# Attention beside a feed-forward block on one core: the normalisation of U moves from VectorE to GpSimd, V in two copies, 36 exp blocks, a new order

## The chip, the cores and the metric

The kernel runs on 1 core of one Trainium2 chip. The metric is the time of one execution on the device in microseconds (us), median of 3 runs. A core has five engines that matter here: TensorE (matmuls into PSUM, an accumulator memory of 8 banks), ScalarE, VectorE, GpSimd and SyncE (which issues most DMAs). In the profile they are PE, ACT, DVE, POOL and SP; PEld is the loading of weights into TensorE.

## What is computed

The input x has 2048 rows of 640. It is normalised over its rows, and the result xn goes into two branches: attention with 32 heads of 20 that share one key and one value head, and a feed-forward block of width 1728 with SiLU. Both are added to x.

```python
def _A_ref(x, wq, wk, wv, wo):
    B, S, D = x.shape
    H = 32
    Dh = D // H
    q = (lambda x, *d: x.transpose(*d))((x @ wq).reshape(B, S, H, Dh), 0, 2, 1, 3)
    k = x @ wk
    v = x @ wv
    scores = jnp.einsum("bhqd,bkd->bhqk", q, k) * (Dh ** -0.5)
    p = _softmax(scores, axis=-1)
    o = jnp.einsum("bhqk,bkd->bhqd", p, v)
    return (lambda x, *d: x.transpose(*d))(o, 0, 2, 1, 3).reshape(B, S, H * Dh) @ wo
...
xn = _layernorm(x, axis=-1)
return x + _A_ref(xn, A_wq, A_wk, A_wv, A_wo) + _B_ref(xn, B_w1, B_w2)
```

## The kernel before

**Blocks, groups, steps.** The scores are computed transposed, in blocks of 128 keys by 512 queries of one head. There are 4 stages of 512 queries, 32 heads and 16 blocks of keys: 2048 blocks. Four heads form a group (32 groups in all, g), and the four heads of a group stand on four tiles of 32 rows of TensorE's array, so that four small matmuls run side by side. A score step (do_S, matmuls on L1127) makes three or four blocks, each in a PSUM bank of its own.

**Two ways to take the exponential.** ScalarE reads one, two or three neighbouring banks in one instruction (L1161) and writes exp to blocks of the buffer E, of which there are NBLK = 35. VectorE reads one bank (L1176) and uses a linear approximation: added to an offset and stored as a 16-bit integer, the score becomes the bit pattern of a bf16 number Z that is close to the exponential. One such reading is coarse, so three are averaged: Z itself and Z with its bits shifted by 43 and by 86, weighted 1, 0.8046875 and 0.625. The two shifts are integer additions on GpSimd (INT64_ADD, L1202, in flush_z), over up to ZB = 3 blocks in one instruction; they write to Y, which has 4 places of two. The weights lie in V, which therefore stands in three copies.

**Weighted sums.** do_pv (L968) multiplies the blocks by V, four tiles side by side, and accumulates a group in one PSUM bank. A block from ScalarE is one matmul; a block from VectorE is three, one for each of its readings. V has one column more that gives the sum of the weights.

**End of a group.** VectorE copies the bank to U (L1245), SyncE transposes U with a DMA to UT (L1216, norm_dma), and normalise takes the reciprocals of the sums on VectorE (L1231) and multiplies (L1236, 128x320) into o. For the last of the 32 groups the transpose is done on TensorE instead. When a stage's groups are done, DMAs on SyncE transpose o to oT (try_oT) for the output projection.

**The rest.** Queries, feed-forward and output projections run as jobs between the score steps (mm4, L870). The hidden layer takes a tanh on ScalarE (L1336) and a product on VectorE (L1341); sums are read on L1405, L1412, L1424. In the opening x is loaded and normalised, keys and values are projected, and VectorE writes the copies of V (L1804, one instruction for each copy and each four row tiles). GpSimd's memsets prepare V (L1597, L1599).

**The order.** All instructions are put in order when the program is built, by a planner (Sched and step) that gives each operation a duration and takes on each engine the ready one of lowest priority number. Each engine then works strictly in that order and waits on semaphores. For an operation of n numbers that VectorE reads from PSUM the planner counts n/960 + 0.067 us, also for the multiplication of normalise; for an addition of n blocks on GpSimd YP_FIX + YP_BLK n. A table SEG holds 64 rows of planner settings, one for each 32 blocks. Among them are thresholds of VectorE's backlog below which it gets one or two blocks of a step (DVE_TH, DVE_TH2) and TILE_CAP, the most blocks of one tile (one head of a group) that VectorE may get.

Of the kernel before, what the change touches and what calls it, by code (L numbers as in the profile page):

```python
# [45 lines left out]
PH = ((0, 1.0), (43, 0.8046875), (86, 0.625))  # L46
# [4 lines left out]
NBLK = 35  # L51
# [53 lines left out]
YP_FIX = 0.147  # L105
YP_BLK = 0.218
# [13 lines left out]
            "ACT4", "SPLIT", "U2", "LOOK", "W4", "M3")  # L120
SEG = (
# [105 lines left out]
class Sched:  # L227
    def __init__(self, nc, stack):
# [12 lines left out]
        self.lock_end = {"dve": 0.0, "pool": 0.0}  # L241
        self.busy = defaultdict(float)
        self.last_add = None
        self.dmaq = defaultdict(float)

    def sem(self, name):
        self.nsem += 1
# [1635 lines left out]
```

## Time and profile before

| | us |
|---|---|
| median of 3 runs | 669.36 |
| lowest and highest | 669.29, 669.47 |
| the profiled execution's own time | 669.12 |
| its span, from the first to the last instruction | 667.3 |

The profile is of one execution. A group of instructions is shown as: line, engine, operation, what it writes and reads (partitions x numbers), count, total busy us, mean ns of one, and then the engine's idle time before them with what ended it. The view by stage gives, for stretches of the span, each engine's busy us with the count of its instructions, the granted clock of TensorE, the share of time in which the DMA engines were busy, and GB/s. The view of waits gives who waited for whom. The chain of waits is followed back from the last instruction and lists start, duration and what it was.

| line | engine | what |
|---|---|---|
| L1127 | PE | score matmuls |
| L1161 | ACT | exp readings |
| L1176 | DVE | exp readings by integers |
| L1202 | POOL | the two shifts of these |
| L968 | PE | weighted sums |
| L870 | PE | projections and feed-forward |
| L1236 | DVE | U times the reciprocals |
| L846 | PE | filling matmuls while nothing else is ready |

### The profile page before, as it was taken

The numbers are of one execution on the slowest core, as the hardware profiler recorded it, in microseconds if no ns is written. First come the engines' busy times: TensorE is split into PE (matmuls) and PEld (weight loads), VectorE is DVE, ScalarE is ACT, GpSimd is POOL, SyncE is SP. The second block draws the span as 40 slices with busy tenths as digits, with TensorE's granted clock in tenths as the row PEclk, the third lists the DMA queues.
The fourth block names the chain that finished last, engine by engine and source line by source line (L and its number), as shares of the span: only waits on it lengthen the run. The fifth ranks groups of instructions, "written<-read, shape, count | busy, mean of one in ns | idle before, by whom it ended". The sixth has DMA issues, their size and how long they took to land.

```text
span 667.3 us, 22800 instructions
## 1 busy us (share of the span) xinstructions
PE 659.4 (99%) x9735; PEld 220.4 (33%) x9735; DVE 601.3 (90%) x1085; ACT 647.7 (97%) x737; POOL 404.6 (61%) x509
## 2 busy tenths in 40 slices
PE   8999999999999999999999999999999999999998
PEld 4432233332323322233333323233233333223345
DVE  7888999999989999999889999988999999998783
ACT  7999999999999999999999999999999999999993
POOL 2056457777486656676556653866767674676550
PEclk9999999999999999999999999999999999999999
DMA  7565201010012210000003110000002121001001
GB/s 211 110 213 150 73 14 12 2 26 2 18 44 62 57 10 17 3 10 18 19 10 84 41 32 17 10 10 18 10 13 47 38 57 37 10 10 31 5 11 41
DMA packets 51433, 26.73 MB, mean 40 GB/s; under 512 B 38566, under 2 KB 50694, under 8 KB 51334
## 3 DMA queue, kind: packets, MB, share of 16 engines
q1 hardware_dynamic: 51190, 25.12, 14.5%
q8 instruction: 78, 1.28, 0.8%
q14 instruction: 21, 0.17, 0.1%
q10 hardware_dynamic: 144, 0.16, 0.1%
HBM read 11.44 MB, written 2.62 MB: 21 GB/s over the span
## 4 chain that ended last, share of the span: by engine, by line
PE 87%; ACT 7%; DVE 3%; SPq 1%; DMA 1%; issue 0%; ACTq 0%
PE psall L968 33%; PE psall L1127 28%; PE psall L870 26%; ACT sbt L1161 6%; DVE sbt L1176 2%; ACT sbt L1336 1%; SPq L1531 1%; DMA sbt<-in_A_x_dram 1%; DVE sbt L1424 0%; PE psall L1326 0%; DVE sbt L1236 0%; ACT sbt L1620 0%; DVE sbt L1666 0%; DVE sbt L1771 0%; ACT sbt L1655 0%
## 5 line engine op out<-in xcount | busy, mean ns | idle before, releaser
L1161 ACT ACTIVATE sbt<-psall 128x1024 bf16<-128x1024 f32 (+2 forms) x649 | 620.1, 1129 | 3.5 <-PE psall L1127 2.6
L1202 POOL INT64_ADD sbt<-sbt x492 | 399.7, 827 | 244.4 <-DVE sbt L1176 171.3
L1176 DVE TENSOR_SCALAR sbt<-psall 128x512 uint16<-128x512 f32 x732 | 473.1, 683 | 46.3 <-PE psall L1127 37.1
L968 PE MATMUL psall<-sbt 128*32 128x512 bf16 x3512 | 265.0, 383 | 0.2
L1127 PE MATMUL psall<-sbt 32*128 32x512 bf16 x2048 | 245.8, 384 | 2.1 <-ACT sbt L1161 0.7
L870 PE MATMUL psall<-sbt 128*32 128x320 bf16 (+2 forms) x3923 | 220.7, 331 | 0.5 <-DVE sbt L1176 0.4
L1127 PEld LDWEIGHTS psall<-sbt 32*128 32x128 bf16 x2048 | 61.9, 91 | 241.4 <-ACT sbt L1161 161.1
L870 PEld LDWEIGHTS psall<-sbt 128*32 128x32 bf16 x3923 | 84.6, 95 | 84.6 <-issue 54.4
L968 PEld LDWEIGHTS psall<-sbt 128*32 128x32 bf16 x3512 | 64.4, 95 | 101.3 <-issue 64.6
L1336 ACT ACTIVATE sbt<-psall 128x512 bf16<-128x512 f32 x54 | 39.6, 739 | 0.0
L1341 DVE SCALAR_TENSOR_TENSOR sbt<-sbt,psall 128x512 bf16<-128x512 bf16 x54 | 36.6, 682 | 2.6 <-ACT sbt L1336 1.2
L1245 DVE CAST sbt<-psall 128x512 bf16<-128x512 f32 x32 | 21.8, 681 | 5.4 <-PE psall L968 5.3
L1236 DVE TENSOR_TENSOR sbt<-sbt 128x320 bf16<-128x320 bf16 x31 | 18.3, 591 | 0.1
L846 PE MATMUL psall<-sbt 128*128 128x512 bf16 (+4 forms) x55 | 15.2, 428 | 1.2 <-DVE sbt L1590 1.2
L1424 DVE SCALAR_TENSOR_TENSOR sbt<-psall,sbt 128x320 bf16<-128x320 f32 x28 | 13.1, 477 | 2.9 <-PE psall L870 2.9
L1405 DVE SCALAR_TENSOR_TENSOR sbt<-psall,sbt 128x320 bf16<-128x320 f32 x28 | 13.5, 483 | 1.6 <-PE psall L870 1.4
L1294 DVE TENSOR_SCALAR sbt<-psall 128x512 bf16<-128x512 f32 (+1 forms) x19 | 12.9, 680 | 0.1
L1635 DVE BATCH_NORM_STATS2 sbt<-sbt 128x6 f32<-128x320 bf16 x22 | 10.0, 470 | 0.9 <-DMA sbt<-in_A_x_dram 0.7
L1421 ACT ACTIVATE sbt<-psall 128x320 bf16<-128x320 f32 x4 | 1.7, 438 | 8.7 <-PE psall L870 8.7
L846 PEld LDWEIGHTS psall<-sbt 128*128 128x128 bf16 x55 | 5.5, 109 | 9.1 <-issue 4.0
L1231 DVE RECIPROCAL sbt<-sbt 128x16 f32<-128x16 bf16 x31 | 7.5, 243 | 0.0
L1620 ACT ACTIVATE sbt<-sbt 128x640 bf16<-128x640 bf16 x5 | 3.6, 730 | 3.2 <-DMA sbt<-in_A_x_dram 3.2
(57 smaller groups left out, 70.1 us busy)
## 6 DMA issues: line engine op xcount, KB each, us to landing
sbt<-in_A_x_dram SPq DMA_DIRECT2D x32, 160.0 KB, 3.2
out_dram<-sbt SPq DMA_DIRECT2D x15, 160.0 KB, 2.0
sbt<-in_B_w_dram SPq DMA_DIRECT2D x5, 432.0 KB, 5.3
sbt<-sbt SPq DMA_DIRECT2D x105, 20.0 KB
sbt<-in_B_w_dram SPq DMA_DIRECT2D x13, 160.0 KB, 3.1
sbt<-sbt SPq DMA_TRANSPOSE x58, 2.5
sbt<-in_A_wo_dram SPq DMA_DIRECT2D x5, 160.0 KB, 3.1
sbt<-in_A_wq_dram SPq DMA_DIRECT2D x5, 140.0 KB, 3.1
```

The lines of the kernel that those rows point to most:

```text
L846: return pe.matmul(self.bk(b, 0, n), self.zero[:, 0:P], self.zero[:, 0:n], start=True, stop=True)
L870: ins = pe.matmul(self.bk(b, 0, n, r, r + SLOT), w[:, r:r + SLOT], x, start=start, stop=stop, tile_position=(0, r), skip_group_check=True)
L968: ins = pe.matmul(self.bk(ub[k], 0, QW, r, r + SLOT), self.v[:, it.w, it.kt, :], it.x(), start=f, stop=False, tile_position=(0, r), skip_g ...
L1127: ins = pe.matmul(self.bk(bank[x]), self.kT[r:r + SLOT, kt * P:(kt + 1) * P], self.qT[r:r + SLOT, g % QS, :], start=True, stop=True, tile_ ...
L1161: return a.activation(self.E[:, b0 * QW:(b0 + na) * QW].rearrange("p (b n) -> p b n", n=QW), src, AF.Exp, scale=ACT_SCALE)
L1176: return v.tensor_scalar(self.Z[:, zs, zp * QW:(zp + 1) * QW], self.bk(bb), OFF, ZMAX, ALU.add, ALU.min)
L1202: sc.new("pool", YP_FIX + YP_BLK * n, lambda g, k=k: g.int64_add(self.Y[:, ys, k, 0:w].bitcast(I64), self.Z[:, zs, 0:w].bitcast(I64), PH[k ...
L1236: sc.new("dve", t_dve_ps(16 * DH), lambda v: v.tensor_tensor(dst, ut[:, :, :, 0:DH], rb, ALU.mult), [key, ("rL", up)], [("o", h0 + i) for ...
L1245: sc.new("dve", t_dve_ps(QW), lambda v: v.tensor_copy(self.U[:, up, :], self.bk(ub)), [("B", ub)], [("U", up)], prio=U_PRIO, name=f"Uev{g}")
L1336: sc.new("act", t_act(QW), lambda a: a.activation(t, src, AF.Tanh, scale=0.5), [("B", b)], [("tb", tp)], prio=TH_PRIO, name=f"th{c}_{fk}") ...
L1341: sc.new("dve", t_dve_ps(QW), lambda v: v.scalar_tensor_tensor(out=self.hT[0:rows, fk, :], in0=t, scalar=1.0, in1=src, op0=ALU.add, op1=AL ...
L1405: sc.new("dve", t_dve_ps(320), lambda v: v.scalar_tensor_tensor(out=in1, in0=ps, scalar=0.5, in1=in1, op0=ALU.mult, op1=ALU.add), [("B", b ...
```

## The change

The three weights become two: both shifted readings have the weight 0.71875, their shifts are 39 and 82, and V stands in two copies. E gets one block more. The multiplication in normalise goes to GpSimd for all groups but the last, at priority 3.0, ahead of the additions at 4.0, with a planned duration of 1.0 us. Additions are planned at 0.159 + 0.222 n us in place of 0.147 + 0.218 n. There is new code that adds the two shifted readings to each other with an accumulating DMA, so that a block from VectorE has two matmuls in place of three; it is taken where GpSimd's planned backlog is under MG, and MG is a new column of SEG, 0 in all its rows. All 64 rows of SEG are new; the last of each is shown. The column TILE_CAP sums to 457 over the rows before and to 431 after; among these stand two values of 21 before and one after.

```diff
-PH = ((0, 1.0), (43, 0.8046875), (86, 0.625))
+SHIFT = (39, 82)
+VW = (1.0, 0.71875)
+NRM = 1.0
+NRM_PRIO = 3.0
...
+ACC_NEXT = (0.28, 0.22, 0.12)
+ACC_FROM = 78.0
+ACC_DMA = 0.0
+MG = 3.0
+MG_END = 16
...
-NBLK = 35
+NBLK = 36
...
-YP_FIX = 0.147
-YP_BLK = 0.218
+YP_FIX = 0.159
+YP_BLK = 0.222
...
-            "ACT4", "SPLIT", "U2", "LOOK", "W4", "M3")
+            "ACT4", "SPLIT", "U2", "LOOK", "W4", "M3", "MG")
...
-    (5.183, 0.388, 0.712, 0.335, 4, 1, 7, 2.4, 0.05, 2.683, 2.77, 8, 2.29, 0.835, 10, 7, 5, 54, 40, 33, 2, 0.2, 1, 0, 99, 0, 0, 1),
...
+    (7.286, 1.014, 0.096, 0.071, 1, 3, 1, 2.27, 0.05, 1.514, 2.65, 30, 2.29, 0.835, 10, 5, 25, 54, 30, 99, 99, 0, 1, 2, 12, 0, 0.5, 2, 0),
...
+        if e == "pool":
+            if op.dma:
+                self.after_acc = 0
+            else:
+                if self.after_acc < len(ACC_NEXT):
+                    op.dur += ACC_NEXT[self.after_acc]
+                self.after_acc += 1
...
-        self.v = sb([P, 3, KT, SLOT], BF16)
+        self.v = sb([P, 2, KT, SLOT], BF16)
...
+        g1 = self.zblocks[-1][1]
+        back = max(sc.t["pool"] - sc.t["pe"], 0.0) + sum(o.dur for o in sc.pend["pool"])
+        merge = n == ZB and back < MG and sc.t["pe"] > ACC_FROM and self.bp < GB * (g1 + 1) - MG_END
...
-                PH[k + 1][0] * 0x0001000100010001), zk + [("lib",)], [("Y", ys, k, i) for i in range(n)],
+                SHIFT[k] * 0x0001000100010001), zk + [("lib",)], [("Y", ys, k, i) for i in range(n)],
...
+        if merge:
+            op = sc.dma("pool", lambda g: g.dma_start(
+                self.Y[:, ys, 0, 0:w].bitcast(BF16), self.Y[:, ys, 1, 0:w].bitcast(BF16), accum_op=ALU.add),
...
-            for k in range(2):
-                self.item(g, j, kt, k + 1, lambda k=k, i=i: self.Y[:, ys, k, i * QW:(i + 1) * QW].bitcast(BF16),
-                          [("Y", ys, k, i)])
+            for k in range(1 if merge else 2):
+                self.item(g, j, kt, 1,
+                          lambda k=k, i=i: self.Y[:, ys, k, i * QW:(i + 1) * QW].bitcast(BF16), [("Y", ys, k, i)])
...
-        sc.new("dve", t_dve_ps(16 * DH), lambda v: v.tensor_tensor(
+        pool = g < self.NG - 1
+        sc.new("pool" if pool else "dve", NRM if pool else t_dve_ps(16 * DH), lambda v: v.tensor_tensor(
             dst, ut[:, :, :, 0:DH], rb, ALU.mult), [key, ("rL", up)], [("o", h0 + i) for i in range(4)],
-            prio=U_PRIO if g < self.NG - 1 else -1.0, name=f"nrm{g}")
+            prio=NRM_PRIO if pool else -1.0, name=f"nrm{g}")
...
-        for k in range(3):
-            pool(0.15, lambda g, k=k: g.memset(self.v[:, k, :, DH:DH + 1], 0.5 * PH[k][1]), [("v0",)],
+        for k in range(2):
+            pool(0.15, lambda g, k=k: g.memset(self.v[:, k, :, DH:DH + 1], 0.5 * VW[k]), [("v0",)],
...
-                for k in range(3):
+                for k in range(2):
                     sc.new("dve", 0.07 + m * DH / 960.0, lambda v, k=k: v.tensor_scalar(
-                        self.v[:, k, n0:n1, 0:DH], sv, PH[k][1], None, ALU.mult),
+                        self.v[:, k, n0:n1, 0:DH], sv, VW[k], None, ALU.mult),
```

More of the change, by code (lines that the diff above doesn't have):

```diff
@@ L45 @@
 OFF = 16045.0
-PH = ((0, 1.0), (43, 0.8046875), (86, 0.625))
+SHIFT = (39, 82)
+VW = (1.0, 0.71875)
+NRM = 1.0
+NRM_PRIO = 3.0
+ACC_ISSUE = 0.9
+ACC_LAND = 5.7
+ACC_RATE = 165e3
+ACC_NEXT = (0.28, 0.22, 0.12)
[3 more added lines that the diff above has]
+MG_END = 16
 ZMAX = 32512.0
@@ L244, in __init__ @@
         self.dmaq = defaultdict(float)
+        self.after_acc = 99
     def sem(self, name):
@@ L319, in commit @@
             else:
-                op.avail = max(op.end + 2.0, q + op.mode / 375e3) + op.late
+                op.avail = max(op.end + 2.0, q + op.mode / (ACC_RATE if op.name == "acc" else 375e3)) + op.late
             self.dmaq[e] = max(q, op.avail - op.late)
@@ L594, in steps_init @@
         self.yset = 0
+        self.merged = 0
+        self.acc_no = [0] * NY
+        self.acc_sem = [self.sc.sem(f"acc{i}") for i in range(NY)]
         self.zblocks = []
@@ L1203, in flush_z @@
                 self.Y[:, ys, k, 0:w].bitcast(I64), self.Z[:, zs, 0:w].bitcast(I64),
-                PH[k + 1][0] * 0x0001000100010001), zk + [("lib",)], [("Y", ys, k, i) for i in range(n)],
+                SHIFT[k] * 0x0001000100010001), zk + [("lib",)], [("Y", ys, k, i) for i in range(n)],
                 prio=4.0, name=f"yp{k}")
+        if merge:
+            op = sc.dma("pool", lambda g: g.dma_start(
+                self.Y[:, ys, 0, 0:w].bitcast(BF16), self.Y[:, ys, 1, 0:w].bitcast(BF16), accum_op=ALU.add),
+                [("Y", ys, 1, i) for i in range(n)], [("Y", ys, 0, i) for i in range(n)], P * w * 2,
+                sem=self.acc_sem[ys], prio=3.9, name="acc")
+            op.dur = ACC_ISSUE
+            op.late = ACC_LAND - 2.0 - ACC_ISSUE
+            self.acc_no[ys] += 1
+            op.inc_no = self.acc_no[ys]
+            self.merged += 1
+            for _, g, kt, j in self.zblocks:
+                self.nz[g][j] -= 0.5
         for i, (t, g, kt, j) in enumerate(self.zblocks):
-            for k in range(2):
-                self.item(g, j, kt, k + 1, lambda k=k, i=i: self.Y[:, ys, k, i * QW:(i + 1) * QW].bitcast(BF16),
-                          [("Y", ys, k, i)])
+            for k in range(1 if merge else 2):
+                self.item(g, j, kt, 1,
+                          lambda k=k, i=i: self.Y[:, ys, k, i * QW:(i + 1) * QW].bitcast(BF16), [("Y", ys, k, i)])
             self.g_late[g] -= 1
@@ L1306, in consume @@
                 ops[-1].dur = 0.74
+                ops[-1].late = ACC_DMA if sc.t["pe"] > ACC_FROM else 0.0
             sc.note(ops[-1], (), [("q", c, h, lo) for h in heads])
```

126 rows, old and new, of the table SEG are left out of this document.

## The prediction

> **What bounds the kernel now.** I read the page's busy shares first, then the busy time by stage, then the waits, and last the chain of waits in one stretch.
>
> ```profile
> PE 659.4 (99%) x9735; PEld 220.4 (33%) x9735; DVE 601.3 (90%) x1085; ACT 647.7 (97%) x737; POOL 404.6 (61%) x509
> ```
> ```profile
> core 0: us, PE busy (x) PEld busy (x) DVE busy (x) ACT busy (x) POOL busy (x), PEclk, DMA share, GB/s
> ...
> 20.00:40.00 20.00, 18.56 (x214) 7.88 (x212) 16.84 (x51) 20.00 (x21) 4.88 (x6) 1.00 0.69 189
> ...
> 200.00:300.00 100.00, 99.72 (x1457) 30.81 (x1447) 95.88 (x163) 99.45 (x114) 66.41 (x82) 1.00 0.12 27
> 300.00:400.00 100.00, 99.92 (x1548) 33.13 (x1542) 90.28 (x153) 99.60 (x106) 62.11 (x77) 1.00 0.13 34
> ...
> 640.00:668.00 28.00, 24.24 (x525) 13.12 (x513) 13.74 (x28) 15.27 (x20) 6.64 (x8) 1.00 0.07 26
> ```
>
> In the long middle TensorE and ScalarE are both occupied over 99% at a granted clock of 1.00, VectorE 90 to 96%, GpSimd 62 to 66%. A busy TensorE can still hide gaps, so the waits come next. Columns: total us, times, longest.
>
> ```profile
> PE psall L846 <- DVE sbt L1590: 1.2, 1, 1.2
> ...
> PE psall L1779 <- DMA sbt<-sbt: 0.2, 1, 0.2
> ```
> ```profile
> PEld psall L1127 <- ACT sbt L1161: 161.1, 414, 0.6
> PEld psall L1127 <- DVE sbt L1176: 57.2, 147, 0.5
> ```
> ```profile
> ACT sbt L1421 <- PE psall L870: 8.7, 1, 8.7
> ...
> ACT sbt L1161 <- PE psall L1127: 2.6, 7, 0.6
> ```
>
> TensorE's own list runs from 1.2 us down to 0.2: nothing to win there. The exp readings (L1161) waited 2.6 us in all; the 8.7 us is the tail. The weight loads of the score step (L1127) name whose bank came free last: ScalarE's 414 times, VectorE's 147 times, so about a quarter of 561 steps start on a bank that VectorE emptied. What is TensorE's full time made of? The chain:
>
> ```profile
> 301.24 0.33 PE psall L1127 x4
> 301.57 0.95 PE psall L870 x20
> 302.52 0.32 PE psall L1127 x3
> 302.85 0.52 PE psall L870 x12
> 303.37 0.32 PE psall L1127 x3
> 303.69 0.66 PE psall L870 x16
> 304.35 0.33 PE psall L1127 x4
> 304.67 1.06 PE psall L870 x28
> ```
> ```profile
> 299.94 0.22 PE psall L968 x4
> ```
>
> Piece follows piece without a hole, all on TensorE. A score step takes 0.32 us whether it makes three blocks or four. Twelve feed-forward matmuls (three sets of four) take 0.52, sixteen 0.66: a set is 0.14, and 0.52 - 3 x 0.14 = 0.10 is lost once on returning from a score step. A score step thus costs 0.32 + 0.10 = 0.42 us, and four weighted sums (L968) cost 0.22. The order is work-conserving: TensorE always has something to do, so the kernel shortens only if the work on TensorE and that on ScalarE both shrink.
>
> **The prices.**
>
> ```profile
> L1161 ACT ACTIVATE sbt<-psall 128x1024 bf16<-128x1024 f32 x565 | 543.3, 1112 | 2.4 <-PE psall L1127 1.4 <-PE psall L968 0.3
> L1176 DVE TENSOR_SCALAR sbt<-psall 128x512 uint16<-128x512 f32 x732 | 473.1, 683 | 46.3 <-PE psall L1127 37.1
> L1202 POOL INT64_ADD sbt<-sbt x492 | 399.7, 827 | 244.4 <-DVE sbt L1176 171.3 <-PE psall L968 69.5 <-PE psall L1127 1.6
> L968 PE MATMUL psall<-sbt 128*32 128x512 bf16 x3512 | 265.0, 383 | 0.2
> ...
> L1161 ACT ACTIVATE sbt<-psall 128x1536 bf16<-128x1536 f32 x51 | 76.3, 1526 | 1.1 <-PE psall L1127 1.1
> ...
> L1236 DVE TENSOR_TENSOR sbt<-sbt 128x320 bf16<-128x320 bf16 x31 | 18.3, 591 | 0.1
> ...
> L1804 DVE TENSOR_SCALAR sbt<-psall 128x80 bf16<-128x80 f32 x12 | 2.8, 233 | 0.1
> ...
> L1597 POOL MEMSET sbt<- 128x1536 bf16 x1 | 1.4, 1379 | 0.0
> ...
> L1747 POOL MEMSET sbt<- 128x640 bf16 x1 | 0.6, 633 | 0.0
> ...
> L1595 POOL MEMSET sbt<- 128x240 bf16 x2 | 0.6, 299 | 0.5 <-DVE sbt L1588 0.5
> ```
> ```profile
> L1236 DVE TENSOR_TENSOR sbt<-sbt x31: 471/483/1072, 60.8 to 640.3; 128x320 bf16<-128x320 bf16 x31
> ```
>
> A block read by ScalarE costs it 1112/2 = 0.556 us (in threes 0.509). A block read by VectorE costs VectorE 0.683 and, shifted twice on GpSimd, goes into three weighted sums instead of one: 2048 + 2 x 732 = 3512, the count of L968. The two extra cost TensorE 2/4 x 0.22 = 0.11 us.
>
> **The normalisation moves.** 31 of the 32 multiplications of L1236 leave VectorE: 18.3 us off. The same view in its by-line form shows their spread, 471/483/1072 ns (least, median, most), so some take twice the median. GpSimd gets 31 of them. None stands on it in this trace. From below: memsets of 240 and 640 elements take 299 and 633 ns, 0.84 ns an element, so 320 elements take 0.37 us, and that only writes. From above: the slowest on VectorE, 1.07 us. I take 0.83, an INT64_ADD, the one GpSimd row that reads tiles and writes one: 31 x 0.83 = 25.7 us (11.5 to 33.2). What hides it: GpSimd was idle 244.4 us before its adds, mostly waiting for VectorE. It goes from 404.6 to some 430 us busy, 64%. If that cover failed, the adds queued behind it are late, and behind them the weighted sums of L968: the slower rival below. VectorE's reciprocal (L1231) stays; the DMAs of a group (the transpose of U) are unchanged in number and queue, and so are the later transposes of o on SP, which now wait for GpSimd. In the tail, the last group keeps VectorE.
>
> The freed VectorE time is worth what it reads: 18.3/0.683 = 26.8 more blocks at most. Best use, taken from step shapes: four steps of two ScalarE blocks and one VectorE block (12 blocks) become three steps of two and two. That is one step less (-0.42), four more weighted sums (+0.22), TensorE -0.20; ScalarE one double less, -1.11; VectorE two more, +1.37. With 26.8/2 = 13.4 of these TensorE loses 2.7 us, ScalarE 14.9. The smaller one counts: **-2.7 us**. Bounds: 0 if the time stays idle; further down if ScalarE's surplus is traded back. Giving z blocks back from VectorE to ScalarE (a double becomes a triple, 1.526 - 1.112 = 0.414) lightens TensorE by 0.11 each; 2.7 + 0.11 z = 14.9 - 0.414 z gives z = 23 and -5.3 us. I take 2.7, since triples need three banks free side by side and today only 51 readings are triples, against 565 doubles.
>
> **The common weight, V in two copies.** Shifts 39 and 82 in place of 43 and 86, one weight 0.71875 for both. The adds and weighted sums keep their number. In the opening four of twelve L1804 go (0.93 us of VectorE), one memset, and a third of the 1.38 us memset: that stage is ScalarE's (20.00 of 20.00 busy) and GpSimd waits there. Between 0 and -0.9 us; I take 0. Beyond VectorE's cover nothing else depends on it.
>
> **36 E blocks.** The room is what V gave up (3 to 2 copies x 16 x 32 = 512 numbers a partition). A reading that waits for a free E block waits for L968, which the waits show as at most 0.3 us in all:
>
> ```profile
> ACT sbt L1161 <- PE psall L968: 0.3, 1, 0.3
> ```
>
> 0 to -0.3; I take 0, as its use lies in freer choices of the order.
>
> **The merge.** The new code could join the two shifted readings with an accumulating DMA, but only if the backlog is under MG, and each of the 64 rows of the new table sets MG to 0; a backlog is never negative. No such DMA is issued, and the terms after it (ACC_NEXT, ACC_DMA) do nothing. Cost 0. Adds are planned at 0.159 + 3 x 0.222 = 0.825 us instead of 0.801, against 0.827 in the trace, so the plan follows GpSimd better. It also loses an error: it counted 0.40 us for the multiplication, against 0.591.
>
> **The order built anew.** No row prices it. Summed over the 64 rows, the cap on VectorE blocks per tile goes from 457 to 431; without the open ones (21, twice before and once after) from a mean of 6.69 (415/62) to 6.51 (410/63), over 128 tiles (four in each of 32 groups) 128 x 0.18 = 23 blocks fewer if the cap always decides. That would be TensorE -2.5 us (23 x 0.11) and ScalarE +12.8 (23 x 0.556). Taken at 0, with both ends kept.
>
> Sum: span 667.3 - 2.7 = 664.6; around it lie 669.12 - 667.3 = 1.8 in the profiled execution, so 666.4. That execution is 0.2 under the median of 669.36; against the median the forecast is **666.6**.
>
> **Rivals.** *The relief stays unused.* VectorE had 46.3 us idle before its readings already, 37.1 of them for want of scores; 18 more change nothing if the caps hold: 669.4. For it the lower caps, against it the 147 steps that VectorE released.
>
> *ScalarE alone is the bound.* Then all 14.9 us are won: 654.5. The chain speaks against it, as TensorE has no hole, and one in the list of waits would show. The Trainium skill, in Perfetto Trace Analysis, section Identifying the Most-Contended Engine, holds that matmul busy time is no measure of headroom and that the share of weight loads is. By that rule the 33% of PEld would leave TensorE free and this rival would be the forecast; the chain above disagrees.
>
> *GpSimd's queue (slower).* GpSimd works in order. Its multiplication waits for a transpose and for VectorE's reciprocal; two adds behind it, 1.65 us, and the weighted sums in TensorE's fixed order then come late. It decides from 2.7/31 = 0.09 us of TensorE stall a group. With 0.2 us a group, 31 x 0.2 = 6.2, net +3.5: 672.9. For it: today's adds start up to VectorE's pace. Against: 244.4 us of idle time, about 1 us before each pair. The Trainium skill speaks against the move: GPSIMD Engine Reference, section Engine selection, has two-input elementwise work about twice as slow there. By that, twice the median would be an estimate of 0.97 us, inside the bounds above, and the chance stays.
>
> *ScalarE gets more blocks (slower).* If the lower caps bring 23 blocks to ScalarE and triples make up for only half, it lengthens by 6.4 us, less the 2.7 that the steps give: +3.7, 673.1. It decides from about five blocks (5 x 0.556 = 2.8).
>
> **How the numbers follow.** Forecast 0.54 (its own range 663.8 to 668.0), unused 0.15, ScalarE alone 0.06, GpSimd's queue 0.13, ScalarE's blocks 0.12. Within 0.2%, 1.3 us, counts as no change; so faster 0.60, same 0.15, slower 0.25. The range 661.5 to 672.0 leaves out the ScalarE case, the worse half of the two slower ones and a little below the forecast.
>
> **What would show it.** Right: L1236 gone from VectorE but for one, 31 TENSOR_TENSOR on GpSimd near 0.8 us, fewer score steps, more of them with four blocks, TensorE and ScalarE still over 99% in the middle. Wrong: TensorE's list of waits with GpSimd or L1202 in whole microseconds; as many steps as before with VectorE lower; more ScalarE readings; or any packets of an accumulating DMA.

## The result: 1006.79 us, and the profile after

The changed kernel takes 1006.79 us (median of 4 runs, 1005.24 to 1009.01) against 669.33 us for the kernel before in the same session: a ratio of 1.5045, with a 95% interval of 1.5012 to 1.5078. The forecast was 666.6, with a range of 661.5 to 672.0.

The page of the changed kernel, busy time of the engines:

```profile
span 1006.0 us, 23004 instructions
...
PE 727.9 (72%) x9752; PEld 227.3 (23%) x9755; DVE 597.0 (59%) x1060; ACT 658.0 (65%) x768; POOL 427.2 (42%) x551
```

VectorE, ScalarE and GpSimd have about the work they had (601, 648 and 405 us before), yet no engine is full. The time by stage shows that this is so from start to end, and that TensorE's clock is lower too. After the stage and its length come PE, PEld, DVE, ACT, POOL, the granted clock, the DMA share and GB/s:

```profile
20.00:40.00 20.00, 17.75 (x203) 7.93 (x202) 15.65 (x46) 19.67 (x19) 4.44 (x6) 1.00 0.71 192
...
200.00:300.00 100.00, 70.85 (x993) 21.46 (x990) 59.66 (x102) 65.47 (x72) 44.95 (x57) 0.85 0.09 24
300.00:400.00 100.00, 74.55 (x999) 22.57 (x995) 62.23 (x102) 69.51 (x79) 38.80 (x50) 0.85 0.06 15
...
980.00:1006.00 26.00, 22.93 (x508) 13.13 (x504) 9.74 (x20) 11.34 (x15) 5.58 (x8) 0.95 0.08 28
```

Whoever looks only at busy shares finds no culprit, since GpSimd shows 42%. The waits of the changed kernel find it (total us, times, longest; the list of TensorE and that of GpSimd):

```profile
PE psall L990 <- POOL sbt L1227: 262.7, 45, 12.8
PE psall L1407 <- POOL sbt L1274: 6.2, 1, 6.2
PE psall L868 <- DVE sbt L1629: 1.2, 1, 1.2
```
```profile
POOL sbt L1227 <- issue: 164.5, 28, 6.3
POOL sbt L1227 <- DVE sbt L1198: 155.3, 103, 28.6
POOL sbt L1274 <- issue: 153.2, 21, 9.6
```

TensorE (weighted sums, now L990) waits 263 us for GpSimd's adds (now L1227). GpSimd's own idle is not all want of work (the 155 us for VectorE): "issue" is time in which nothing that the profile shows was awaited, 5.9 us on average before an add (164.5/28) and 7.3 us before a multiplication (153.2/21). One group in order of time, GpSimd alone:

```profile
205.48 0.82 POOL L1227 INT64_ADD sbt<-sbt  x1 [0.75 <-PE psall L1149]
213.65 0.72 POOL L1274 TENSOR_TENSOR sbt<-sbt 128x320 bf16<-128x320 bf16 x1 [7.34 <-issue]
220.07 5.62 POOL L1227 INT64_ADD sbt<-sbt  x7 [5.71 <-issue]
```

Before the 0.72 us of the multiplication lie 7.3 us of nothing, and behind it 5.7. What stands there is seen by asking for the line of the multiplication and for that of the add (least/median/most ns):

```profile
L1274 POOLq MODIFY_POOL_CONFIG  x62: 1/11/13, 54.4 to 968.9; - x62
L1274 POOL TENSOR_TENSOR sbt<-sbt x31: 717/717/720, 64.1 to 976.4; 128x320 bf16<-128x320 bf16 x31
```
```profile
L1227 POOLq MODIFY_POOL_CONFIG  x62: 1/1/3, 65.0 to 977.4; - x62
```

Two MODIFY_POOL_CONFIG stand before each of the 31 multiplications, and two before the first add behind it. The source names neither: the finished program has them wherever GpSimd goes from the code set of the 64-bit add, which load_lib loads in the opening, to TENSOR_TENSOR and back. They take nanoseconds themselves; that the loading behind them takes the microseconds is the theory tested below. The kernel before has a single such pair, in the opening:

```profile
L1579 POOLq MODIFY_POOL_CONFIG  x2: 13/13/13, 1.5 to 1.6; - x2
```

Its first add stood at 32.55 us, 0.1 us behind the end of the reading that it waited for (L1176, 31.75 + 0.69), so no loading held it up there. The multiplication itself is as short as forecast, and VectorE gets ten blocks more (742 against 732).

```profile
L1183 ACT ACTIVATE sbt<-psall 128x1024 bf16<-128x1024 f32 x554 | 534.7, 1057 | 293.6 <-PE psall L1149 292.4
L1198 DVE TENSOR_SCALAR sbt<-psall 128x512 uint16<-128x512 f32 x742 | 483.4, 684 | 376.7 <-PE psall L1149 370.2
L1227 POOL INT64_ADD sbt<-sbt x504 | 400.8, 807 | 340.2 <-issue 164.5 <-DVE sbt L1198 155.3 <-PE psall L990 18.8
...
L1274 POOL TENSOR_TENSOR sbt<-sbt 128x320 bf16<-128x320 bf16 x31 | 22.2, 717 | 223.0 <-issue 153.2 <-DVE sbt L1198 41.9 <-PE psall L1149 14.2
```

GpSimd's idle before the multiplications is 223.0/31 = 7.2 us each; only its label varies with what else was awaited meanwhile. With 5.9 behind each, GpSimd loses 31 x 13.1 = 406 us.

### The profile page after: what moved, and what is told of

The parts are those of the page before. It is cut to its first block, busy times and chain, and to the rows that moved or that the text cites. A ratio compares the mean times of both kernels' runs of the same rounds, so it can differ in the third digit from the quotient of the medians.

```text
span 1006.0 us, 23004 instructions
## 1 busy us (share of the span) xinstructions
PE 727.9 (72%) x9752; PEld 227.3 (23%) x9755; DVE 597.0 (59%) x1060; ACT 658.0 (65%) x768; POOL 427.2 (42%) x551
## 4 chain that ended last, share of the span: by engine, by line
PE 59%; issue 22%; ACT 8%; POOL 6%; DVE 5%; SPq 1%; DMA 0%; POOLq 0%
PE psall L990 24%; PE psall L1149 19%; PE psall L892 15%; ACT sbt L1183 7%; POOL sbt L1227 4%; DVE sbt L1198 4%; POOL sbt L1274 1%; ACT sbt L1375 1%; SPq L1570 1%; DMA sbt<-in_A_wq_dram 0%; SPq L1600 0%; PE psall L1818 0%; DVE sbt L1332 0%; PE psall L1365 0%; PE psall L1407 0%
## 5 line engine op out<-in xcount | busy, mean ns | idle before, releaser
L1183 ACT ACTIVATE sbt<-psall 128x1024 bf16<-128x1024 f32 (+2 forms) x680 | 627.9, 1037 | 330.6 <-PE psall L1149 329.2
L1198 DVE TENSOR_SCALAR sbt<-psall 128x512 uint16<-128x512 f32 x742 | 483.4, 684 | 376.7 <-PE psall L1149 370.2
L1227 POOL INT64_ADD sbt<-sbt x504 | 400.8, 807 | 340.2 <-issue 164.5
L990 PE MATMUL psall<-sbt 128*32 128x512 bf16 x3532 | 312.8, 434 | 263.1 <-POOL sbt L1227 262.7
L1149 PE MATMUL psall<-sbt 32*128 32x512 bf16 x2048 | 262.2, 413 | 2.9 <-ACT sbt L1183 0.9
L990 PEld LDWEIGHTS psall<-sbt 128*32 128x32 bf16 x3532 | 68.6, 98 | 397.2 <-POOL sbt L1227 301.8
L1274 POOL TENSOR_TENSOR sbt<-sbt 128x320 bf16<-128x320 bf16 x31 | 22.2, 717 | 223.0 <-issue 153.2
L892 PEld LDWEIGHTS psall<-sbt 128*32 128x32 bf16 x3923 | 84.9, 96 | 87.0 <-issue 53.4
L1375 ACT ACTIVATE sbt<-psall 128x512 bf16<-128x512 f32 x54 | 37.4, 698 | 0.0
L1444 DVE SCALAR_TENSOR_TENSOR sbt<-psall,sbt 128x320 bf16<-128x320 f32 x28 | 13.6, 486 | 3.2 <-PE psall L892 3.1
L1463 DVE SCALAR_TENSOR_TENSOR sbt<-psall,sbt 128x320 bf16<-128x320 f32 x28 | 13.1, 481 | 2.6 <-PE psall L892 2.6
L1818 PE MATMUL psall<-sbt 128*128 128x256 bf16 x40 | 5.9, 274 | 0.2 <-DVE sbt L1198 0.2
```

The lines of the kernel that those rows point to most:

```text
L892: ins = pe.matmul(self.bk(b, 0, n, r, r + SLOT), w[:, r:r + SLOT], x, start=start, stop=stop, tile_position=(0, r), skip_group_check=True)
L990: ins = pe.matmul(self.bk(ub[k], 0, QW, r, r + SLOT), self.v[:, it.w, it.kt, :], it.x(), start=f, stop=False, tile_position=(0, r), skip_g ...
L1149: ins = pe.matmul(self.bk(bank[x]), self.kT[r:r + SLOT, kt * P:(kt + 1) * P], self.qT[r:r + SLOT, g % QS, :], start=True, stop=True, tile_ ...
L1183: return a.activation(self.E[:, b0 * QW:(b0 + na) * QW].rearrange("p (b n) -> p b n", n=QW), src, AF.Exp, scale=ACT_SCALE)
L1198: return v.tensor_scalar(self.Z[:, zs, zp * QW:(zp + 1) * QW], self.bk(bb), OFF, ZMAX, ALU.add, ALU.min)
L1227: sc.new("pool", YP_FIX + YP_BLK * n, lambda g, k=k: g.int64_add(self.Y[:, ys, k, 0:w].bitcast(I64), self.Z[:, zs, 0:w].bitcast(I64), SHIF ...
```

## The experiments

The theory to be tested, A: changing GpSimd's code twice a group costs it 13 us, the adds come late, and TensorE waits. The copy with code changes, the eight changes, the move in the kernel before and both orders around the true price have a single run each; the other times are medians of 4 runs, that of the copy of 11. Rivals: B, such work on GpSimd stalls it by itself; C, the new order, the common weight or the 36 blocks are at fault.

**A copy in place of the multiplication.** All engines keep their order; only GpSimd's operation differs.

```diff
-        sc.new("pool" if pool else "dve", NRM if pool else t_dve_ps(16 * DH), lambda v: v.tensor_tensor(
+        sc.new("pool" if pool else "dve", NRM if pool else t_dve_ps(16 * DH), lambda v: v.tensor_copy(dst, ut[:, :, :, 0:DH]) if pool else v.tensor_tensor(
             dst, ut[:, :, :, 0:DH], rb, ALU.mult), [key, ("rL", up)], [("o", h0 + i) for i in range(4)],
```

> The changed kernel with its order untouched; only the multiplication of the 31 groups on GpSimd is replaced by a plain copy of the same 128x320 numbers, so the division by the sum of the weights is left out. Theory A (code loading: the GpSimd code of the 64-bit add and that of TENSOR_TENSOR are not resident together, and each change between them costs some 6 to 7 us of GpSimd): a copy needs no change, the two MODIFY_POOL_CONFIG in front of each go away, and the time falls to 668 to 675 us at a clock near 1.00. Theory B (any SBUF work of VectorE's kind on GpSimd in that place stalls it, by its ports or its late place in the queue): stays over 950 us. Theory C (the new order, the common weight or the 36 blocks are at fault): stays at about 1007 us.

Measured: 669.51 us against 669.42, ratio 1.0003 (0.9994 to 1.0012), clock 1.00. The whole loss is gone. Page and, by line, the copy of this run:

```profile
PE 657.3 (98%) x9752; PEld 220.7 (33%) x9755; DVE 592.1 (89%) x1060; ACT 645.9 (97%) x768; POOL 419.3 (63%) x551
```
```profile
L1274 POOL COPY sbt<-sbt x31: 448/449/451, 54.7 to 639.6; 128x320 bf16<-128x320 bf16 x31
```

GpSimd does 31 operations on the same tiles at the same places in the queue, and nobody is late. So B falls for the place and the tiles, and C falls. The run shows a second thing: with VectorE relieved and no loading, all of the change together is worth nothing, neither way; it doesn't part the terms from one another.

**The copy, with code changes around it.**

```diff
+        def copy_between_loads(v):
+            v.load_library(library_config.all_libraries[0])
+            ins = v.tensor_copy(dst, ut[:, :, :, 0:DH])
+            v.load_library(library_config.all_libraries[1])
+            return ins
```

> As the run with the copy (the division by the sums is left out in 31 groups), but with an explicit change of GpSimd's code to the standard set before each copy and back to the set of the 64-bit add behind it. Theory A: the changes alone bring the loss back, 980 to 1030 us, with gaps of 6 to 7 us before the copy and before the next add, and no TENSOR_TENSOR on GpSimd but none is needed. Theory B, that TENSOR_TENSOR itself is what stalls: as without the changes, 668 to 680 us.

Measured: 1007.36 us, clock 0.84. By line and by waits of TensorE:

```profile
L1275 POOL COPY sbt<-sbt 128x320 bf16<-128x320 bf16 x31 | 13.7, 441 | 227.5 <-issue 135.9 <-DVE sbt L1198 69.4 <-DVE sbt L1385 14.1
```
```profile
PE psall L990 <- POOL sbt L1227: 260.3, 46, 12.6
```

No TENSOR_TENSOR runs on GpSimd here, and gap (227.5/31 = 7.3 us), wait and time are those of the changed kernel. The changes of code alone make the loss; what is left of B falls too.

**Eight changes, and one.** The edit is that of the copy, with `pool and g % 4` and then `pool and g != 12` as its condition, so that 8 groups and 1 group still multiply.

> The changed kernel in the same order, with the multiplication on GpSimd in eight of the 31 groups (every fourth) and a copy in the other 23, where the division by the sums is left out. Theory A with a loss that adds up: 8/31 of the loss of 337 us, 87 us, so 757 us (735 to 775); with a granted clock between the two. If the loss were one global state (a lower clock once GpSimd stalls at all), it would lie near 1000 us; if a single stall is absorbed by the order's reserves, below 720 us.

> The changed kernel in the same order with the multiplication on GpSimd in one group of the middle (g = 12) and a copy in the other 30, where the division by the sums is left out. Theory A: one change to and fro, GpSimd gone for some 13.5 us; TensorE waits for 7 to 10 us of it, and little is lost by the clock: 677 to 682 us against 669.5 with none. If the loss adds up exactly as over 31 groups: 680.4 us. If the order's reserves take one stall: under 672 us.

Measured: 764.75 us with eight, 682.61 with one (ratio 1.0194, 1.0177 to 1.0211). Over the 669.51 of none, that is 95.2 us or 11.9 each, and 13.1 for one, against 10.9 each for all 31. In these runs the loss adds up, a little less than in proportion. The upper end expected for a single change, 682, was passed by 0.6 us. Waits of TensorE, first with eight, then with one:

```profile
PE psall L990 <- POOL sbt L1227: 74.8, 9, 11.4
```
```profile
PE psall L990 <- POOL sbt L1227: 10.5, 1, 10.5
```

With one change the kernel loses 13.1 us, as much as GpSimd loses to loading, and TensorE waits 10.5 of them in one piece: the order has next to no reserve for it.

**The kernel before with this one move.** Same edit in the kernel before (planned 1.0 us on GpSimd), with its own weights, three copies of V, 35 blocks and settings.

> The kernel before with one change: the multiplication of the 31 groups goes to GpSimd, planned at 1.0 us; weights, V, 35 blocks and settings stay. Theory A (GpSimd's code is changed twice a group): the same loss as the whole change, 980 to 1030 us. If the new order or the two copies of V took part in it: clearly less, under 900 us.

Measured: 1011.31 us, clock 0.84. The move alone brings the whole loss, and nothing else of the change is needed for it. TensorE's waits:

```profile
PE psall L968 <- POOL sbt L1202: 269.0, 40, 12.9
```

**The multiplication back on VectorE.**

```diff
-        pool = g < self.NG - 1
+        pool = False
```

The priority of the multiplication is put back too (U_PRIO).

> The changed kernel with the multiplication back on VectorE; common weight, two copies of V, 36 blocks and the new settings stay, and the planner orders it with them. Theory A: no change of code after the start, so no loss of hundreds of us; the planner's own sum for this order is 10 us above that of the kernel before, so 675 to 685 us. If the relief of VectorE by 18 us is worth what the prediction's step shapes gave (2.7 us), no more than 673 us.

Measured: 679.54 us, ratio 1.0155 (1.014 to 1.017). Without loading the clock is 1.00 again, and the page shows an order that is only less fitting:

```profile
PE 664.5 (98%) x9726; PEld 222.5 (33%) x9729; DVE 599.9 (89%) x1076; ACT 655.2 (97%) x779; POOL 401.8 (59%) x512
```

ScalarE has 7.5 us more to do than before, in 779 instructions where it had 737, TensorE 5.1 us more. The settings were chosen for an order with the multiplication elsewhere, so this run doesn't price the 36 blocks by themselves.

**The order built around the true price.** NRM = 13.6 in place of 1.0; then the same without the filling matmuls after the opening.

```diff
-NRM = 1.0
+NRM = 13.6
```

> The changed kernel with one number of the planner altered: the multiplication on GpSimd is planned at 13.6 us (7 of change, 0.7 of work, 5.8 of change back) in place of 1.0, so the order is built around the true price, and TensorE gets filling matmuls in the gaps. Theory A: GpSimd is busy or loading 31 x 13.6 + 401 = 823 us, and the time is 870 to 910 us; the clock comes back to above 0.95, since TensorE no longer idles. If only the order's ignorance of the price were the trouble: near 700 us. If the price were wrong: still about 1000 us.

> The order built around the true price (13.6 us a multiplication), but without the filling matmuls after the opening. The planner's own sum moves by 3.5 us. If the idle of TensorE lowers its granted clock, as the changed kernel's 0.84 suggests, the clock falls from 0.97 to below 0.93 and the time rises by 15 to 60 us over the 881 with them, 895 to 940 us. If the clock had another cause (GpSimd's loading, say): clock and time as with the filling, 880 to 890 us.

Measured: 881.33 us at a clock of 0.97 with fills; 883.34 at 0.874 without. An order that knows the price saves 125 us. It can hardly save more with this work on GpSimd, by the sum of 31 x 13.6 planned and 394 of adds, 816 us. The second half of the expectation for the run without fills was wrong: the clock fell below 0.93, but the time did not follow. The page of each, with fills first:

```profile
PE 816.9 (93%) x10344; PEld 291.6 (33%) x10347; DVE 592.2 (67%) x1051; ACT 668.2 (76%) x784; POOL 420.6 (48%) x543
```
```profile
PE 724.5 (82%) x9746; PEld 249.8 (28%) x9749; DVE 596.0 (68%) x1057; ACT 666.4 (76%) x777; POOL 423.1 (48%) x549
```

Here TensorE has time to spare (82% busy without the fills), and slower matmuls can fill it. The planner ordered the two differently (496 and 502 adds) and each ran once, so they don't price the clock.

**Does the low clock cost anything in the changed kernel?** In sums over TensorE, its wait for GpSimd (262.7 + 6.2) and the growth of its own work against the run with copies (727.9 - 657.3 = 70.6) make 339.5, about the difference of the spans, 1006.0 - 668.1 = 337.9. But such a sum doesn't show that the 70.6 cost time. Around the wait of the group shown above, by stages of the changed kernel:

```profile
208.00:220.00 12.00, 2.01 (x26) 0.44 (x22) 2.48 (x4) 3.19 (x4) 0.72 (x1) 0.79 0.00 1
220.00:225.00 5.00, 4.06 (x35) 0.79 (x35) 1.76 (x3) 1.50 (x2) 4.93 (x7) 0.50 0.01 3
225.00:230.00 5.00, 5.00 (x77) 1.42 (x69) 4.15 (x8) 4.56 (x6) 3.74 (x6) 0.99 0.00 0
```

The wait ends at 220.94, and TensorE then runs for some 4 us at half its clock: 35 matmuls in 4.06 us, then 77 in 5.00. To tell whether that costs anything, matmuls with zeros were put into the waits; they change no sum and no order.

```diff
+                        def fill36(pe, fb=fb):
+                            for _ in range(36):
+                                ins = pe.matmul(self.bk(fb, 0, QW, 0, SLOT), self.zero[:, 0:SLOT], self.zero[:, 0:QW], start=False,
+                                                stop=False, tile_position=(0, 0), skip_group_check=True)
+                            return ins
```

> The changed kernel with its order untouched and 36 matmuls with zeros (36 x 0.213 = 7.7 us) put on TensorE ahead of the first weighted sum that needs an add from behind a multiplication, once a group. They add nothing to the sums and run while TensorE would wait for GpSimd. In the changed kernel TensorE waited 263 us for GpSimd and its own work took 71 us more than in the run with copies, at a clock of 0.84. If the 71 us are the price of the lower clock, and idle lowers it: clock above 0.93, 940 to 985 us. If the lower clock costs no time here, as in the order built around the true price: 1000 to 1015 us with a higher clock. If loading GpSimd's code lowers the clock: clock still near 0.84 and 1005 us or more.

> As the run with 36 matmuls with zeros, with 18 (3.8 us a group). In the run with 36, twelve or so of the 31 fills ended with no wait behind them, so some of them were too long, and their overrun can hide a gain by the clock; 18 fit into nearly every wait. If the lower clock is part of the loss (own work of TensorE 71 us over the run with copies): clock 0.89 to 0.94 and 975 to 997 us. If GpSimd's changes set the time and TensorE's slower work hides in it: within 3 us of the changed kernel, 1003 to 1010 us, TensorE's own work shrinking and its wait growing by as much.

> The changed kernel with its order untouched; the fills with zeros in front of the first weighted sum behind each multiplication are now as long as TensorE's wait in that very place was in the changed kernel, less 0.9 us: between 10 and 58 matmuls, 1137 in all (243 us of its 263 us of waits), none at two places without a wait. No fill should outlast its wait by much, and TensorE goes from each fill to its work nearly without a pause. If the low clock behind each wait is part of the loss: clock above 0.95, TensorE's own work back by 40 to 70 us and the time at 935 to 975 us. If GpSimd sets the time whatever TensorE's speed is: 1000 to 1012 us.

| run | clock | zeros, us | wait for the adds, us | TensorE's own work, us | time, us |
|---|---|---|---|---|---|
| changed kernel | 0.841 | 0 | 262.7 | 727.9 | 1006.79 |
| 36 everywhere | 0.966 | 246.1 | 55.9 | 687.5 | 1007.86 |
| 18 everywhere | 0.907 | 125.6 | 147.8 | 716.1 | 1009.25 |
| as long as each wait | 0.996 | 250.3 | 24.3 | 670.0 | 967.85 |

(Own work is TensorE's busy time without the zeros. The time is the median of four runs, the rest is of the profiled execution.) The first two gave nothing, and by them alone the low clock would have been declared harmless. With 36 everywhere own work shrank by 40.4 us, but zeros and remaining waits sum to 302.0, 39.3 more than the 262.7 of waits before: some zeros outlasted their wait and took back what the clock gave. With 18 the rest of a wait lay behind the zeros; own work shrank by only 11.8 us, and zeros and waits sum to 273.4, 10.7 more. With a length for each place the clock stayed up and 38.9 us were won. Page of this run:

```profile
PE 920.3 (96%) x10889; PEld 333.4 (35%) x10892; DVE 595.7 (62%) x1060; ACT 655.8 (68%) x768; POOL 426.7 (44%) x551
```
```profile
PE psall L1011 <- POOL sbt L1248: 24.3, 56, 1.2
```

So of the loss of 337 us at least some 39 are the low clock that the waits bring; the other 298 are put down to the late adds, though a part of them may be clock that this filling did not win back. TensorE's own work shrank by 57.9 us, but zeros and waits together grew by 11.9 (274.6 against 262.7), and the profiled executions differ by 42.5 (1006.0 and 963.5).

## Why the prediction was wrong

- **The price of the move** is the step that failed. The prediction put it: "I take 0.83, an INT64_ADD, the one GpSimd row that reads tiles and writes one", between 0.37 and 1.07. The instruction takes 0.717, inside the bounds. But the price of an instruction isn't the price of the place in which it stands: it came with 7.2 us of loading before it and 5.9 behind, some 18 times itself. The bounds were drawn around rows of instructions, and no row of the kernel before has a change of GpSimd's code in its middle. INT64_ADD was not the one such row either: TENSOR_SCALAR_AFFINE_SELECT (L1584, 128x128, 0.297 us) reads a tile and writes one too. What could have been seen is the explicit load of a code set in the opening (L1579 and its two MODIFY_POOL_CONFIG) and that behind it GpSimd runs only INT64_ADD, memsets and that one AFFINE_SELECT at 2.26 us, and no TENSOR_TENSOR.
- **GpSimd's queue**, the slower rival, had the right chain: adds queued behind the multiplication, weighted sums behind them, TensorE waiting. Its size was 0.2 us a group; measured were 10.9. The chance of 0.13 went with that size. The first of the prediction's signs of being wrong, TensorE waiting for GpSimd in whole microseconds, is what came.
- **The Trainium skill was cited by the right page and another section than the one that mattered.** The Trainium skill, GPSIMD Engine Reference, section Instruction dispatch, has the first call to freshly loaded code pay about 6 us (5.95) with no visible instruction. This case agrees on the way back (5.9 us before the add) and shows more before the multiplication (7.2 to 7.3). The rule that the prediction did cite, twice the time for two-input work, would have made an estimated 0.97 us; 0.717 against VectorE's median of 0.483 is 1.48 times.
- **-2.7 us by VectorE's relief** did not come, even without the loading: 669.51 against 669.42 with copies. VectorE got 10 blocks more and not 26.8, and ScalarE has 90 single readings where it had 33, with 36 triples for 51. The prediction took the sum of 414 and 147 for the number of score steps, but these are the times that a step's weight loads waited for ScalarE or VectorE; in the run with copies they are 424 and 142 (the rows below). Counted in the traces as unbroken runs of score matmuls, the steps are 626 before and 623 with copies, 171 and 179 of them with four blocks: three steps fewer, where 13.4 were forecast. What kept the relief from doing more is not shown, since it came together with new settings and lower caps. With the multiplication back on VectorE the time was 10.0 us longer than with copies, but in an order built anew. By its time the run with copies is the rival "the relief stays unused", under the loss.

```profile
PEld psall L1149 <- ACT sbt L1183: 167.6, 424, 0.9
...
PEld psall L1149 <- DVE sbt L1198: 54.7, 142, 0.4
```

- **Right**: the merge is never taken (no accumulating DMA in the trace; the queue q10 has its 144 packets as before); the two copies of V and the weight cost nothing that shows in the run with copies; GpSimd's own work, 427.2 us against some 430 forecast; ScalarE and TensorE are full together, as the run with copies shows again (97% and 98%).
- **Not tried**: other settings for the multiplication on VectorE with 36 blocks, which could tell what the added block is worth; and any version that beats the kernel before. The copies show that GpSimd's help, even free, would not have made one with this order.

## What to carry to other kernels

Before an operation goes to GpSimd, ask which code set it needs and which one stands there: here one change to and fro costs GpSimd 13 us, as much as 18 of the multiplications that it was made for, and shows only as GpSimd's idle time, most of it labelled "issue". Copies and memsets ran here beside the 64-bit add with no change; TENSOR_TENSOR did not. A planned order believes its prices, so one wrong price can return as a wait wherever it was used (45 waits here), and a single trial of one instance (here +13.1 us) would have shown it.

## What was not expected of the hardware

- TensorE comes out of a wait of some 11 us at half its clock for some 4 us (0.50, then 0.99 in the stages above). The Trainium skill, TensorE: Matmul & The Clock Gate, Part 1, puts the warming at about 3.4 us of sustained work, and the trace agrees with its order of size.
- Zeros in a wait helped here only where they lasted nearly to its end: 18 or 36 at each place won nothing, 10 to 58, measured for each place, 39 us.
- A lower clock need not show in the time: at 0.874 the kernel took 883.34 us, at 0.973 with fills 881.33, one run each of two orders in which GpSimd is loaded or busy for some 816 us.
